# Loading and scaling of q, sums of tokens and scaling of v at the opening of a kernel's second level

## The chip, the core and the metric

The kernel runs on one core of a Trainium2 chip. The metric is the time of one execution on the device in microseconds (us), as the median of several runs. TensorE (PE; its weight loads PEld) multiplies and transposes, VectorE (DVE) and GpSimd (POOL) do arithmetic on tiles, ScalarE (ACT) copies and scales, SyncE (SP) issues DMAs. ScalarE and GpSimd also issue DMAs from their own queues. Each engine works through its own queue in order.

## The reference

Eight batches of eight heads, 576 tokens, 64 numbers a head; a retention block without softmax, and on its result a feed-forward block whose two branches are multiplied. All in float32.

```python
scores = scale * np.matmul(q, k.transpose(0, 1, 3, 2))
ret = scores * Dmat            # gamma_h ** (s - t) for t <= s, else 0
attn = np.matmul(ret, v)
x = attn.transpose(0, 2, 1, 3).reshape(B * S, H * D)   # 4608 x 512
a, b = x @ w1, x @ w2                                  # 512 x 1024 each
out = ((a * b) @ w3) @ w_out                           # 1024 x 1024, 1024 x 512
```

The decay is split: q is multiplied by gamma_h ** s / 8 and k's side (here v) by gamma_h ** -t before the products, so only a triangular mask is left for the scores.

## The kernel before

**Units of attention.** A unit `g` is a pair of batches (`i`) and a piece of the tokens (`c`): five pieces, the first of 64 tokens and four of 128, so 20 units; `NC` is 5. For each unit q and k are needed transposed (`qT`, `kT`), as 128 x (2 x 4 x 128) tiles; `score` (L233, L236) makes the masked scores, `state` (L255) adds k and v into a running state, `pv` (L274, L299) makes 128 columns of x, still transposed (`xT`).

There are two ways to `qT`. By **blocks**: `load_blocks` (L171) issues on SP up to 16 DMAs per unit, each of 32 KB, in runs of 32 numbers (128 bytes), so that every 32 x 32 block lies where a DVE block transpose finds it; `scale_blocks` (L181) multiplies by the decay on POOL in two instructions; `front_blocks` (L190) transposes on DVE. By **natural rows**: `load` (L93) issues one DMA in runs of 64 numbers (256 bytes); `scale` multiplies by the decay on POOL (L204) or head by head on ScalarE (L202, eight instructions); `front` transposes on TensorE (L218), eight instructions per tensor, into two PSUM tiles, which ScalarE copies out (L221).

**Feed-forward.** w3 @ w_out is multiplied out once (`w3o`). The products are Strassen-like (seven products for eight). Batches 0 to 3 use one level for the up products (`up`). From unit 10 on a second level is used: `up2(gr, n)`, 14 steps (`n` from 0 to 13) for each of four groups of two thirds-of-a-pair. I number the steps of a group from 1. A step is seven products of four matmul instructions each (L1035) on one weight form, which is fetched from HBM into a ring of three slots (`ra<-kept`, L939) by `next_forms`, mostly from POOL, two steps ahead. PSUM results go to the running sums `cc` by ScalarE copies (L1049, L1054, L1058, L1065), DVE sums (L1045, L1047) and POOL sums (`more`, L1040). Half-way through each step one entry of the list `beside` is run. `down` makes the output: seven products of eight matmul instructions (L637), with sums by DVE (`plus`, L641; S4 at L679; L681); P3, the last, needs S4 and the space of P5.

**Sums of tokens.** `token_forms(gr)` puts ten entries, each of one to three DVE instructions (L951), on a list. They make the second level's operands from `xT`. Step 1 needs the entries up to `outer`, step 3 the second-last, step 5 the last.

**The order of the work** is written out by hand: the program's text is the order on each engine, except that `work(n)` takes n pieces from the list `todo`, and small pieces wait in lists that other work empties: `spread` (one entry after each sum of `down` or `up`, all of them at `flush`), `aside` (after some sums), `beside` (in `up2`), `loads`. Before the second level, `open_second` and every `up2` call `flush`. Before the change, the ten entries for group 0 are on `spread`: four go out in `down` of tiles (2, 2) and (3, 2), and the other six at the `flush` in `open_second`, just ahead of `down` of (3, 0) and (3, 1), which is the last piece before step 1.

**Loops around the change.** After unit 9 there is a written-out passage for unit 10; then a loop over g from 10 to 19, in which `dealt[g - 10]` pieces of work (3, 4, 4, 3, 3, 7, 7, 3, 7, 7) are done, while unit g + 1 is prepared: v scaled by two entries of `beside` (four heads each), q scaled on POOL, q and k transposed after the second-last and last but one of the pieces, loads for g + 2 issued. At the end of the turn `pv(g)`, `state(g + 1)`, `score(g + 1)`. What is left in `beside` goes out before `pv`.

Of the kernel before, what the change touches and what calls it, by code (L numbers as in the profile page):

```python
# [13 lines left out]
ALU = mybir.AluOpType  # L14
# [5 lines left out]
def kernel(  # L20
# [16 lines left out]
    B, H, S, D = q.shape  # L37
# [10 lines left out]
    NC = (S + P - 1) // P  # L48
# [74 lines left out]
    for c in (0, slice(1, NC)):  # L123
        n = short if c == 0 else P
# [440 lines left out]
    aside, owed, spread, beside, loads = [], [], [], [], []  # L565
    g = 0
# [58 lines left out]
    def down(x, y, then=None, last=False):  # L625
        a, done, left = pair_of(x, y)
        second = "first" in live
        ahead(x, y)
        while len(done) < (1 if second else 3):
            aside.pop(0)()  # L630
        ps = {}
        ot = pools["ot"].tile([P, 2, 2, DM // 2], F32, tag="ot", name="ot")

        def product(nm, A, B, on=None):
            ps[nm] = ps[on] if on else acc.tile([P, DM // 2], F32, tag="acc", name="po")
            for f in range(NP):
                nc.tensor.matmul(ps[nm], a[A][:, f, :], live["W"][B][:, f, :], start=(f == 0 and not on),  # L637
                                 stop=(f == NP - 1), skip_group_check=True)

        def plus(nm, to, sb):  # L640
            nc.vector.tensor_add(ot[:, to[0], to[1]], ps[nm], ot[:, sb[0], sb[1]])  # L641
            if spread:
                spread.pop(0)()
            if second and aside and nm != 3:
                aside.pop(0)()

        def put(m, t, row, half=slice(0, 2)):

            i, n = every[m]
            r0 = t * P  # L650
            while r0 < (t + 1) * P:
                b = r0 // TB
                e = min((b + 1) * TB, (t + 1) * P)
                r = (2 * i + b) * S + n * TB + r0 - b * TB
                stores.append((out[r:r + e - r0, half.start * DM // 2:half.stop * DM // 2],
                               ot[r0 - t * P:e - t * P, row, half].rearrange("p h d -> p (h d)")))
                r0 = e
            if not keep_stores and not second:
                store()

        C11, C12, C21, C22 = (0, 0), (0, 1), (1, 0), (1, 1)
        product(1, "A11", "B11")
        first = ot[:, 0, 0]
        if second and steps[0]:
            first = live["first"].pop(0)
            live["first"].append(first)
        nc.scalar.copy(first, ps[1])
        if second:
            store()
            finish()  # L670
        product(7, "S3", "T3")
        if second:
            multiply()
        while len(done) < 3:
            aside.pop(0)()
        if then:
            ahead(*then)
        product(2, "A12", "B21", on=1)
        nc.vector.tensor_tensor(out=a["S4"], in0=a["A12"], in1=a["S2"], op=ALU.subtract)  # L679
        product(6, "S2", "T2")  # L680
        nc.vector.tensor_add(ot[:, 0, 1], ps[6], first)  # L681
        nc.scalar.copy(ot[:, 0, 0], ps[2])
        early = second or last or g >= 2 * NC - 1
        if early:
            put(*x, 0, slice(0, 1))
            store()
        plus(7, C21, C12)
        product(5, "S1", "T1")
        plus(5, C22, C21)
        product(4, "A22", "-T4")  # L690
        plus(4, C21, C21)
        put(*y, 1)
        if second:
            store()
        product(3, "S4", "B22", on=5)
        while aside and not early:
            aside.pop(0)()
        plus(3, C12, C12)
        put(*x, 0, slice(1 if early else 0, 2))
        if last:  # L700
            store()
        while aside:
            aside.pop(0)()

    stores, keep_stores = [], []

    def store():
        while stores:
# [102 lines left out]
    while multiplied[0] < KF:  # L811
# [3 lines left out]
        if todo:  # L815
            first = converted[0] < 4 * NQ
# [88 lines left out]
    def flush():  # L905
        while spread:
            spread.pop(0)()
# [34 lines left out]
    def token_forms(gr):  # L942


        x = [live["xT", m] for m in groups[gr]]
        T, E, U = live["T2"], live["E"], live["U"]
        forms = live["B2", gr] = {}
        names = ("B11", "B21", "B22", "T3", "T1", "T2", "-T4")

        def tt(out, in0, in1, op=ALU.subtract):  # L950
            nc.vector.tensor_tensor(out=out, in0=in0, in1=in1, op=op)  # L951

        b11, b21 = (x[0].rearrange("p (r c) b t -> p r c b t", c=2)[:, :, c] for c in range(2))
        b12, b22 = (x[1].rearrange("p (r c) b t -> p r c b t", c=2)[:, :, c] for c in range(2))

        def first():
            for s in range(2):
                tt(x[s][:, :2, 1], x[s][:, 2:, 1], x[s][:, :2, 1])


        def outer():
            if "E4" not in live:
                live["E4"] = pools["carry"].tile([P, KF, P], F32, tag="carry", name="e4").rearrange(
                    "p f n -> p (f n)")[:, :4 * TB].rearrange("p (r b t) -> p r b t", r=2, b=2)
            E4 = live["E4"]
            tt(E4, b21, E[:, 1])
            for nm, (r, b) in {"B11": (0, 0), "B21": (1, 0), "T3": (0, 1), "B22": (1, 1)}.items():
                parts = (b11, b21, b22, b12, E[:, 0], E[:, 1], E4)
                forms[nm] = dict(zip(names, (y[:, r, b] for y in parts)))

        def pair(k):
            for s in range(2):
                if k == 1:
                    tt(T[:, s, 1], x[s][:, :2, 1], x[s][:, :2, 0], ALU.add)
                else:
                    tt(T[:, s, k], x[s][:, 2:, 1 if k == 0 else 0], T[:, s, 1])

        def inner(k):
            u = [U[j] if k != 2 else (U[3][:, 0], U[3][:, 1], U[4][:, 0])[j] for j in range(3)]
            b11, b21, b12, b22 = (T[:, s, k, c] for s in range(2) for c in range(2))  # L980
            tt(u[1], b12, b11, ALU.add)
            tt(u[0], b22, u[1])
            tt(u[2], b21, u[1])
            for i, nm in enumerate(("T1", "T2") if k != 2 else ("-T4",)):
                part = [y[:, i] if k != 2 else y for y in (b11, b21, b22, b12, *u)]
                forms[nm] = dict(zip(names, part))

        spread.extend([first, lambda: tt(b12, b22, b12), lambda: tt(E[:, 1], b12, b11, ALU.add),
                       lambda: tt(E[:, 0], b22, E[:, 1])])
        spread.extend([lambda: pair(1), lambda: pair(0), lambda: pair(2), outer, lambda: inner(slice(0, 2)),  # L990
                       lambda: inner(2)] if gr else
                      [outer, lambda: pair(1), lambda: pair(0), lambda: pair(2), lambda: inner(slice(0, 2)),
                       lambda: inner(2)])
# [19 lines left out]

    def up2(gr, n):

        flush()
        h, key = n // 7, order[n % 7]
        slot = ring[steps[0] % 3]
        if not steps[0]:
# [108 lines left out]
    g = NC  # L1128
# [9 lines left out]
    for g in first_pair:  # L1138
        n = (1, 1, 2, 2)[g - NC]
# [37 lines left out]

    g = 2 * NC - 1
    work(1)
    load_blocks(g + 1, "q")  # L1180
    pv(g)()
    load(g + 2, "v", nc.scalar)
    load(g + 2, "k")
    scale_blocks(g + 1)
    scale(g + 1, "v")
    open_first()
    token_forms(0)

    g = 2 * NC
    work(1)  # L1190
    aside.append(lambda: front_blocks(g, "q"))
    work(1)
    while aside:
        aside.pop(0)()
    front(g, "k")
    next_forms(nc.scalar)
    ready = {2 * NC + 3: 1, 3 * NC + 1: 2, G - 1: 3}

    whole = range(2 * NC + 1, 2 * NC + 4)
    load_blocks(g + 1, "q")  # L1200
    state(g)
    score(g)
    add_group(0)
# [1 line left out]
    for g in range(2 * NC, G):  # L1205
        n = dealt[g - 2 * NC]
        if g + 1 < G:
            beside.extend(lambda j=j: scale(g + 1, "v", range(j, j + H // 2)) for j in (0, H // 2))
            tail = min(n, 4) - 3
            work(n - 2 - tail)  # L1210
            scale_blocks(g + 1)
            for nm in "qk":
                blocks_in = nm == "q" or g + 1 not in whole
                if blocks_in:
                    aside.append(lambda nm=nm: front_blocks(g + 1, nm))
                work(1)
                while aside:
                    aside.pop(0)()
                if not blocks_in:
                    while loads:  # L1220
                        loads.pop(0)()
                    front(g + 1, "k")
                if g + 2 < G and not (nm == "k" and g + 2 in whole):
                    load_blocks(g + 2, nm)
            work(tail)
            for left in (loads, beside):
                while left:
                    left.pop(0)()
        else:
            work(n)  # L1230
# [14 lines left out]
    g = G  # L1245
# [44 lines left out]
```

## Time and profile before

| | |
|---|---|
| median of 3 runs | 848.06 us (847.11 to 848.5) |
| the profiled execution | 856.03 us |
| its span, first to last instruction | 854.3 us |
| TensorE busy, of the span | 825.4 us (97%) |
| VectorE, ScalarE, GpSimd busy | 547.3, 282.8, 229.8 us |
| mean clock granted to TensorE | 0.988 |
| mean DMA rate | 149 GB/s |

The profile is that of one execution. A line of it names the engine, the line of the kernel, the operation, the tile written and those read (`out<-in`), the shape, the count. Matmuls are pipelined, and their ends are modelled. Times within the execution are counted from its first instruction.

### The profile page before, as it was taken

What the parts mean: (1) busy time and instruction counts of PE and PEld (TensorE: products, weight loads), DVE (VectorE), ACT (ScalarE), POOL (GpSimd) and SP (SyncE); (2) the same over time, 40 slices, a digit from 0 to 9 for tenths busy, and PEclk for the clock granted to TensorE, in tenths of its full rate; (3) what the DMA queues carried; (4) which work ended last, traced back from release to release, by engine and by line L of the source; (5) the groups of instructions that cost most, each with busy time, mean ns of one, the idle gap of its engine ahead of it and who ended that gap; (6) DMA issues with size and microseconds to landing.
All of it is one profiled execution on the core that took longest, in us unless ns stands there. A gap on an engine that the chain in (4) does not pass through costs nothing.

```text
span 854.3 us, 15755 instructions
## 1 busy us (share of the span) xinstructions
PE 825.4 (97%) x6085; PEld 743.0 (87%) x6085; DVE 547.3 (64%) x959; ACT 282.8 (33%) x581; POOL 229.8 (27%) x253
## 2 busy tenths in 40 slices
PE   9899999999999999986999999999999999999998
PEld 8899999644889898876999888999889998899987
DVE  4899999991654477943655862757654657645653
ACT  4787556670111011132453105342024231033300
POOL 1100010001103162203756103746005452035600
PEclk9999999999999999997999999999999999999999
DMA  9995464436046467987876427797446453145401
GB/s 190 217 218 132 76 149 124 126 96 111 1 95 124 74 179 265 262 257 153 236 198 186 100 65 176 229 228 209 77 90 201 158 193 132 49 138 188 167 26 50
DMA packets 201292, 126.96 MB, mean 149 GB/s; under 512 B 161272, under 2 KB 183032, under 8 KB 201216
## 3 DMA queue, kind: packets, MB, share of 16 engines
q1 hardware_dynamic: 170944, 50.14, 29.3%
q0 software_dynamic: 11632, 62.79, 22.7%
q10 hardware_dynamic: 18640, 13.02, 5.5%
q8 instruction: 48, 0.79, 0.4%
q14 instruction: 28, 0.23, 0.1%
HBM read 103.62 MB, written 22.28 MB: 147 GB/s over the span
## 4 chain that ended last, share of the span: by engine, by line
PE 81%; DMA 7%; DVE 6%; issue 3%; SPq 1%; ACT 1%; POOL 1%; ACTq 0%; DVEq 0%; POOLq 0%
PE po L637 23%; PE up L1035 15%; PE seed L1035 12%; PE up L524 12%; PE ps L477 6%; PE xps L299 4%; PE sc L233 3%; PE xps L274 2%; DMA ld_v<-in_v_dram 2%; DMA ra<-kept 2%; DMA raw<-in_moe_w_dram 2%; SPq L171 1%; PE tp L218 1%; DVE c L529 1%; PE st L255 1%
## 5 line engine op out<-in xcount | busy, mean ns | idle before, releaser
L637 PE MATMUL po<-w3o,ab 128*128 128x256 f32 x552 | 126.8, 385 | 5.4 <-DVE ot L641 4.4
L637 PEld LDWEIGHTS po<-w3o,ab 128*128 128x128 f32 x552 | 104.8, 192 | 22.7 <-DVE ot L641 6.7
L1040 POOL TENSOR_TENSOR cc<-cc 128x384 f32<-128x384 f32 x112 | 109.4, 1001 | 5.8 <-ACT cc L1058 4.1
L1047 DVE TENSOR_TENSOR cc<-seed,cc 128x384 f32<-128x384 f32 x88 | 48.7, 553 | 78.1 <-PE seed L1035 63.7
L1035 PE MATMUL up<-xT,ra 128*128 128x192 f32 x384 | 74.9, 332 | 0.5 <-DMA ra<-kept 0.5
L181 POOL TENSOR_TENSOR bl_q<-bl_q,gqs 128x512 f32<-128x512 f32 (+1 forms) x30 | 32.1, 1089 | 154.1 <-DMA bl_q<-in_q_dram 118.5
L1047 DVE TENSOR_TENSOR cc<-up,cc 128x384 f32<-128x384 f32 x88 | 48.5, 551 | 38.8 <-PE up L1035 30.7
L524 PE MATMUL up<-xT,wA 128*128 128x192 f32 x384 | 70.5, 327 | 0.0
L939 POOL DMA_DIRECT2D ra<-kept x53 | 30.0, 567 | 147.7 <-PE seed L1035 126.9
L529 DVE TENSOR_TENSOR c<-up,c 128x384 f32<-128x384 f32 x80 | 44.0, 549 | 39.7 <-PE up L524 39.1
L236 DVE TENSOR_TENSOR pm<-sc,mask 128x512 f32<-128x512 f32 (+1 forms) x80 | 45.4, 627 | 36.9 <-PE sc L233 36.8
L1035 PEld LDWEIGHTS up<-xT,ra 128*128 128x128 f32 x384 | 64.8, 193 | 1.8 <-DMA ra<-kept 0.8
L637 PE MATMUL po<-wB,forms 128*128 128x256 f32 x288 | 65.1, 379 | 0.0
L524 PEld LDWEIGHTS up<-xT,wA 128*128 128x128 f32 x384 | 63.3, 190 | 1.2 <-issue 0.5
L1035 PE MATMUL seed<-e,ra 128*128 128x192 f32 x256 | 52.5, 334 | 9.4 <-DVE cc L1047 6.9
L637 PEld LDWEIGHTS po<-wB,forms 128*128 128x128 f32 x288 | 54.7, 190 | 7.4
L1054 ACT COPY seed<-up 128x384 f32<-128x384 f32 x56 | 26.0, 463 | 96.1 <-PE up L1035 48.7
L1035 PE MATMUL up<-ra 128*128 128x192 f32 x288 | 56.1, 332 | 0.0
L477 PE MATMUL ps<-wo,w3T 128*128 128x512 f32 x128 | 55.1, 592 | 0.0
L1035 PEld LDWEIGHTS seed<-e,ra 128*128 128x128 f32 x256 | 43.0, 192 | 11.9 <-DVE cc L1047 7.2
L477 PEld LDWEIGHTS ps<-wo,w3T 128*128 128x128 f32 x128 | 24.3, 190 | 30.1 <-issue 29.7
L1035 PEld LDWEIGHTS up<-ra 128*128 128x128 f32 x288 | 49.3, 194 | 0.1
(126 smaller groups left out, 1477.5 us busy)
## 6 DMA issues: line engine op xcount, KB each, us to landing
ra<-kept POOLq DMA_DIRECT2D x53, 896.0 KB, 5.0
raw<-in_moe_w_dram SPq DMA_DIRECT2D x72, 128.0 KB, 3.0
bl_q<-in_q_dram SPq DMA_DIRECT2D x216, 32.0 KB, 2.8
out_dram<-ot ACTq DMA_DIRECT2D x54, 128.0 KB, 2.4
bl_k<-in_k_dram SPq DMA_DIRECT2D x136, 32.0 KB, 3.4
raw<-in_moe_w_dram SPq DMA_DIRECT2D x16, 256.0 KB, 6.7
ld_k<-in_k_dram SPq DMA_DIRECT2D x8, 512.0 KB, 5.6
raw<-in_moe_w_out_dram SPq DMA_DIRECT2D x32, 128.0 KB, 2.7
```

Source lines behind the costliest of these rows:

```text
L181: nc.gpsimd.tensor_tensor(out=part, in0=part, in1=gqs[:, :, n0:n0 + n].unsqueeze(3).to_broadcast([P, NP, n, BL]), op=ALU.mult)
L236: nc.vector.tensor_mul(pm[:sz, b, j, :, :sz], sc[j][:sz, :, :sz], mask[:sz, :sz].unsqueeze(1).to_broadcast([sz, NP, sz]))
L299: nc.tensor.matmul(banks[r][heads[half], b, n, :sz], vs[:sz, b * H + 2 * p + j, :], pm[:sz, b, j, p, :sz], start=(c == 0 and m == 0), stop ...
L477: nc.tensor.matmul(ps, live["w3T", ft][:, g, :], live["wo"][:, g, :], start=(g == 0), stop=(g == KF - 1))
L524: nc.tensor.matmul(ps[:, w, :], a[:, w, r, :], b[:, r, :], start=(new and w == r == 0), stop=(w == r == 1), skip_group_check=True)
L529: nc.vector.tensor_add(c[:, to], ps, c[:, sb])
L637: nc.tensor.matmul(ps[nm], a[A][:, f, :], live["W"][B][:, f, :], start=(f == 0 and not on), stop=(f == NP - 1), skip_group_check=True)
L939: engine.dma_start(ring[n % 3], kept[n % 14 // 7][nm])
L1035: nc.tensor.matmul(ps[:, w, :], weight_of(slot, a, w), B[b], start=(new and w == 0), stop=True, skip_group_check=True)
L1040: nc.gpsimd.tensor_tensor(out=o, in0=o, in1=i, op=ALU.add)
L1047: nc.vector.tensor_add(c[:, j], ps, with_add[:, j])
L1054: nc.scalar.copy(p6, p1)
```

## The change

Four edits, all in the order and the place of work; the values computed are the same.

- The ten entries of `token_forms` go on a list of their own, `pieces`. `down` takes one after each sum where `spread` is empty; `open_second` no longer empties them; `up2` leaves at most two before step 1, one before step 2, none before step 3.
- q of unit 10 is loaded by natural rows on SP, scaled on ScalarE (an entry of `aside`, taken in the last `down` before step 1), and transposed on TensorE together with k.
- q of unit 11 likewise; it is scaled by two entries of `beside` in steps 1 and 2, and transposed after step 3 with k.
- In every turn of the loop, the two entries that scale v go on `beside` after the first pieces of work of the turn, not before.

```diff
@@ down, plus @@
             if spread:
                 spread.pop(0)()
+            elif pieces:
+                pieces.pop(0)()
...
-    stores, keep_stores = [], []
+    stores, keep_stores, pieces = [], [], []
...
@@ token_forms @@
-        spread.extend([first, lambda: tt(b12, b22, b12), lambda: tt(E[:, 1], b12, b11, ALU.add),
+        pieces.extend([first, lambda: tt(b12, b22, b12), lambda: tt(E[:, 1], b12, b11, ALU.add),
                        lambda: tt(E[:, 0], b22, E[:, 1])])
-        spread.extend([lambda: pair(1), lambda: pair(0), lambda: pair(2), outer, lambda: inner(slice(0, 2)),
+        pieces.extend([lambda: pair(1), lambda: pair(0), lambda: pair(2), outer, lambda: inner(slice(0, 2)),
                        lambda: inner(2)] if gr else
...
     def up2(gr, n):
 
-        flush()
+
+        while len(pieces) > max(0, 2 - n):
+            pieces.pop(0)()
...
     g = 2 * NC - 1
     work(1)
-    load_blocks(g + 1, "q")
+    load(g + 1, "q")
     pv(g)()
     load(g + 2, "v", nc.scalar)
     load(g + 2, "k")
-    scale_blocks(g + 1)
     scale(g + 1, "v")
...
-    aside.append(lambda: front_blocks(g, "q"))
+    aside.append(lambda: scale(g, "q", True))
     work(1)
     while aside:
         aside.pop(0)()
-    front(g, "k")
+    front(g)
...
-    load_blocks(g + 1, "q")
+    load(g + 1, "q")
...
         if g + 1 < G:
-            beside.extend(lambda j=j: scale(g + 1, "v", range(j, j + H // 2)) for j in (0, H // 2))
+            q_blocks = g > 2 * NC
+            if not q_blocks:
+                beside.extend(lambda j=j: scale(g + 1, "q", range(j, j + H // 2)) for j in (0, H // 2))
             tail = min(n, 4) - 3
             work(n - 2 - tail)
-            scale_blocks(g + 1)
+            beside.extend(lambda j=j: scale(g + 1, "v", range(j, j + H // 2)) for j in (0, H // 2))
+            if q_blocks:
+                scale_blocks(g + 1)
             for nm in "qk":
-                blocks_in = nm == "q" or g + 1 not in whole
+                blocks_in = q_blocks if nm == "q" else g + 1 not in whole
                 if blocks_in:
                     aside.append(lambda nm=nm: front_blocks(g + 1, nm))
                 work(1)
                 while aside:
                     aside.pop(0)()
-                if not blocks_in:
+                if not blocks_in and nm == "k":
                     while loads:
                         loads.pop(0)()
-                    front(g + 1, "k")
+                    front(g + 1, "k" if q_blocks else "kq")
```

## The prediction

> **What bounds the kernel now.** I read the page first: TensorE's busy row, the clock row, the shares of the chain.
>
> ```profile
> PE 825.4 (97%) x6085; PEld 743.0 (87%) x6085; DVE 547.3 (64%) x959; ACT 282.8 (33%) x581; POOL 229.8 (27%) x253
> PEclk9999999999999999997999999999999999999999
> PE 81%; DMA 7%; DVE 6%; issue 3%; SPq 1%; ACT 1%; POOL 1%; ACTq 0%; DVEq 0%; POOLq 0%
> ```
>
> TensorE sets the end; only work taken from it, or a gap closed in it, counts. The one slice at a low clock is the 19th of 40, 384 to 406 us, where the second level opens. So next the busy time by stage (columns: stretch, its length, busy us and count of PE, PEld, DVE, ACT, POOL, clock, DMA share, GB/s): the last `down` before the second level, its first three steps, three later steps (from 404.9), and steps 1 and 2 of unit 15.
>
> ```profile
> 354.90:372.50 17.60, 14.27 (x57) 11.55 (x57) 14.15 (x23) 0.74 (x2) 4.42 (x3) 0.90 0.98 279
> 375.10:399.70 24.60, 17.71 (x87) 16.67 (x85) 5.91 (x12) 7.45 (x19) 7.15 (x8) 0.79 0.71 184
> 404.90:418.80 13.90, 13.90 (x88) 13.75 (x86) 8.71 (x15) 6.71 (x17) 10.34 (x12) 1.00 0.80 219
> 516.70:530.20 13.50, 11.38 (x60) 10.85 (x58) 3.03 (x8) 5.86 (x16) 3.83 (x5) 0.87 0.90 239
> ```
>
> Three steps take 13.90 us where nothing is late, 24.60 at the opening. The timeline of these stretches (start, length, engine, line, operation; in brackets the idle time before it and what ended it) tells why:
>
> ```profile
> 358.57 1.87 DVE L951 TENSOR_TENSOR ra<-xT 128x384 f32<-128x384 f32 x2
> 366.40 0.68 DVE L679 TENSOR_TENSOR ab<-ab,forms 128x512 f32<-128x512 f32 x1
> 368.86 3.68 PE L637 MATMUL po<-w3o,ab 128*128 128x256 f32 x8 [3.31 <-DVE ot L641]
> 372.66 27.75 SPq L171 DMA_DIRECT2D bl_q<-in_q_dram  x39
> 389.20 2.06 POOL L181 TENSOR_TENSOR bl_q<-bl_q,gqs 128x512 f32<-128x512 f32 x2 [26.99 <-DMA bl_q<-in_q_dram]
> 391.83 1.95 POOL L1040 TENSOR_TENSOR cc<-cc 128x384 f32<-128x384 f32 x2
> 392.87 0.56 DVE L1047 TENSOR_TENSOR cc<-seed,cc 128x384 f32<-128x384 f32 x1 [8.22 <-POOL cc L1040]
> 393.48 1.65 PE L1035 MATMUL seed<-e,ra 128*128 128x192 f32 x4 [6.89 <-DVE cc L1047]
> 396.20 2.76 PE L1035 MATMUL up<-ra 128*128 128x192 f32 x8
> ...
> 523.08 1.28 ACT L202 ACTIVATE ld_v<-ld_v,gk 128x128 f32<-128x128 f32 x4 [3.39 <-DMA ld_v<-in_v_dram]
> 525.15 0.95 PE L1035 MATMUL seed<-e,ra 128*128 128x192 f32 x4 [2.12 <-ACT seed L1054]
> 525.90 2.76 PE L1035 MATMUL up<-xT,ra 128*128 128x192 f32 x8
> ```
>
> Stall A (3.31 us): six sums of tokens, flushed together, hold DVE to 366.4; S4 and the sums of `down` queue behind them, and P3 waits for these. Stall B (6.89): POOL's head is the scaling of q of unit 11, whose sixteen block loads SP issues at 0.45 us each, after a stop:
>
> ```profile
> SPq L171 <- DMA ra<-kept: 5.5, 1, 5.5
> ```
>
> Behind it on POOL stand the form's DMA and the `more` sums of step 2; DVE and TensorE wait for those. Stall C (2.12): ScalarE waits for v of unit 16 in step 1, and the copy that seeds step 2 is behind it. After each, the same matmuls cost double for a while.
>
> **What the Trainium skill says.** "TensorE: Matmul & The Clock Gate", What's actually happening: an idle window of about 3.4 us halves the clock, and as much busy time restores it. The trace agrees: eight matmuls take 2.76 us after stalls B and C, 1.46 elsewhere. "SBUF — State Buffer", Who interferes with whom: a DVE instruction with two SBUF inputs is shut out while GpSimd reads SBUF. Here one DVE sum of 128x384 took 2.25 us at 360.4 while POOL scaled v of unit 10, its neighbours 0.55. "DMA: Bandwidth & Descriptors", Why small descriptors are slow: some 3 cycles per packet beside its 32-byte beats, so 256 B in two runs of 128 B cost 14, in one run 11. By that the new loads are about a fifth cheaper, an estimate; the trace has no such pair side by side.
>
> **The change, part by part,** in the profiled execution (856.03 us, span 854.3).
>
> Sums of tokens (A). The six leave 357.7 to 366.4. Four go one after each of the four L641 sums of that `down`, two to the starts of steps 2 and 3, where DVE was idle for 4.68 us before its first sum. POOL no longer scales q or (since its queue isn't blocked from 329 to 357.7) v there, so a dealt pair costs 2 x 0.55. Worked forward: P2 ends 360.4, S4 361.1, L681 at 362.2, sum 7 363.1, `outer` (0.95) 364.0, sum 5 364.4, a pair to 365.5, sum 4 366.0, a pair 367.1. P4 ends at 365.55, and P3 needs S4 and sum 5 only: no stall, and 1.99 instead of 3.68 us. That is 3.31 + 1.69 = 5.0 gained. If the dealt sums run as slowly as under POOL (0.97 each), sum 5 is at 365 and P3 still on time.
>
> q of unit 10. Off: 8 loads on SP (349.9 to 354.8), two scalings on POOL (2.25), one DVE transpose (0.70). On: one load; 8 multiplications by ScalarE after sum 7 (v of 64 rows: 8 in 2.45 us, 512.60 to 515.05), so 363.1 to 365.6, where ScalarE is idle; behind them stand only stores and the copies of `front`. 8 more transposes: the 8 of k took 0.63, so 0.6 on the path; two more copies (0.65), of which about 0.3 shows, since `state` (1.1) covers the rest and `score` wants the second. Cost 0.9. Four `front` tiles and four of `score` turn over five PSUM buffers; sum 3 (367.9) frees the fourth tile's in time. Net to here 4.1: step 1 begins at about 372.1, not 376.2.
>
> q of unit 11 (B). Off: 16 loads, POOL's 2.06, DVE's 1.23. On: one 512 KB load, 8 multiplications in fours (1.28 us) at the middle of steps 1 and 2, 8 transposes, 2 copies. SP's own order is kept, but the 24 loads are now 2; each load on SP or ScalarE waits for the landing of the one eight before it (the landings and issues pair off so in the trace), which was the 5.5 us stop. The load now follows the forms' load directly, at about 368 (the last send waits for the store behind L682, now about 367). k of unit 11, as large and natural, landed in 5.2 us at full DMA; with 1.8 MB of forms beside it I take 7: 375. ScalarE wants it at 372.1 + 3.1 = 375.2. So POOL has only forms and sums, and from the start of step 1 to `front` it takes 3 x 4.55 (a step's distance in the chain after 409.76) less the 0.65 of the product that comes later, 13.0, where it was 376.2 to 399.7, 23.5: 10.5 gained. Cost at the end of the stage: 8 transposes 0.87; ScalarE's four copies (2.3) and v's second half, which moving v one step leaves to after step 3 (1.28), end 4.0 us after `front` begins, when `state` wants v at 1.74 + 1.1 = 2.8: 1.0 more. Cost 1.9. SP then loads q of unit 12 some 12 us earlier; in 368 to 386 DMA has about 4.6 MB to move, 256 GB/s, under the 279 it moved in the first stretch.
>
> v by a step (C). Same eight multiplications, later: steps 2 and 3 of short units, 5 and 6 of those with seven, steps that already held POOL's scaling without loss in units of four. Unit 15: C and its slow clock are 2.12 + 1.95. But the forms of steps 3 and 4 land at 526.12 and 531.78, set by POOL and DMA, not by the wait; so step 4 begins at 531.8 instead of 534.1: 2.3 gained, not 4.1. Unit 18: the trace has step 2 at 5.18 instead of 4.55: 0.6. Unit 16: a form landing at 571.27 bounds it, 0.3.
>
> Sum: 4.1 + 10.5 - 1.9 + 2.3 + 0.6 + 0.3 = 15.9, so 840.1 for the profiled execution. The median of the runs is 848.06; the profiled one has 8 us more, and I can't see where. If a part of that is in these stalls, less is to be had; I take 14 off the median: 834.
>
> **Rivals.**
> R1, ScalarE takes over POOL's wait: q of unit 11 lands at 385, not 375, because two loads of forms share the DMA. For: those took 5.7 and 7.1 us there, and bl_q's first pieces up to 7.3. Against: SP reaches the load earlier, and half as many packets. TensorE then idles some 9.5 us; gain 15.9 - 9.5 = 6.4, so 841.7.
> R2, the runs without a profile hold most of their 8 us less in exactly these stalls: gain 8 to 9, 839.5. Nothing in the trace speaks for or against.
> R3, slower: the same wait on ScalarE, longer. It decides where q lands 15.9 us after ScalarE wants it, at 391 (388 if the slow clock's 3.3 us come on top). The last block of q landed at 389.2 before, so it takes a load as late as the blocks were. At 394 it is about 851. Against: the blocks' lateness was mostly issue and the stop of 5.5, both gone.
> R4, q wasn't the release: POOL is held by another load and B stays; A's gain is eaten by the 1.9 and 0.9. Within 0.2% of 848. Against: the bracket at 389.20 names the load.
>
> **How the numbers follow.** Forecast 834 (829 to 839): 0.62. R2: 0.11. R1: 0.16. R4: 0.03. R3: 0.08. The range to 843 takes in R1 and R2 and leaves out about 0.15. Faster by over 0.2% (what a measurement here can tell): 0.89; same 0.03; slower 0.08.
>
> **What would show it.** A: no gap over 1 us before the last product of the `down` ahead of step 1, its eight matmuls at about 2.0 us. B: POOL's first work after the opening is a form's DMA and `more`; steps 1 to 3 in 14 us; the clock row without its 7. A gap on ScalarE before L202 on ld_q would be R1 or R3. C: no wait for ld_v at L202 in unit 15, but one for ra of about 1 us in TensorE at its steps 3 and 4. I am wrong if step 3 still ends 20 us or more after the seeds, or if a new gap over 2 us stands before `state` of unit 11.

## The result and the profile after

The changed kernel takes 839.28 us (median of four runs) where the kernel before takes 847.72 on the same chip. The gain is 8.4 us; 14 were forecast. One of the four runs, the profiled one, was disturbed (a span of 942.5 us at a clock of 0.846) and is left out of the ratio, which is 0.9891 with a 95% interval of 0.9868 to 0.9914; the median of the other three is 838.87 us.

All that is shown of "after" therefore comes from a second profile of the same kernel, `all_again`: its span is 837.3 us, its own run 838.99 us.

The page of that profile: busy time by engine, the clock row in 40 slices, the shares of the chain.

```profile
PE 819.1 (98%) x6101; PEld 736.9 (88%) x6101; DVE 544.1 (65%) x957; ACT 289.8 (35%) x601; POOL 225.4 (27%) x249
PEclk8999999999999999999999999999999999999999
PE 76%; DMA 10%; DVE 4%; SPq 4%; issue 3%; ACT 2%; POOL 1%; ACTq 0%; DVEq 0%; POOLq 0%
```

The 7 in the clock row is gone, and TensorE has the 16 transposes more that q of two units needs (6101 for 6085). The busy time by stage, with the columns as in the prediction: the last `down`, steps 1 to 3, and the stretch from the transposes of unit 11 to step 4.

```profile
350.90:368.90 18.00, 16.28 (x137) 13.88 (x137) 9.97 (x19) 4.88 (x15) 0.00 (x0) 0.98 0.98 291
371.50:385.40 13.90, 13.54 (x82) 12.98 (x81) 6.01 (x13) 8.47 (x23) 4.77 (x6) 1.00 0.85 198
385.40:392.00 6.60, 6.60 (x114) 5.98 (x112) 2.79 (x6) 4.34 (x11) 1.59 (x2) 1.00 0.61 167
```

Steps 1 to 3 take 13.9 us instead of 24.6, at full clock. POOL does nothing in the `down` (0.00): it has no q to scale there, and v of unit 10, which stood behind q on POOL, is scaled at 328.47 us instead of 359.99. Lines of the timeline of the same kernel (line numbers are two to four higher than before):

```profile
354.98 0.37 ACT L669 COPY ot<-po 128x256 f32<-128x256 f32 x1 [7.93 <-DMA out_dram<-ot]
355.40 1.99 PE L637 MATMUL po<-w3o,ab 128*128 128x256 f32 x8 [0.74 <-ACT ot L669]
...
362.42 1.89 PE L637 MATMUL po<-w3o,ab 128*128 128x256 f32 x8
364.68 1.02 DVE L953 TENSOR_TENSOR ra<-xT,ra 128x384 f32<-128x384 f32 x2
365.32 1.12 ACTq L712 DMA_DIRECT2D out_dram<-ot  x2
366.48 0.65 ACT L221 COPY kT<-tp 128x256 f32<-128x256 f32 x2 [3.49 <-DVE ra L953]
367.46 1.46 PE L233 MATMUL sc<-qT,kT 64*64 64x64 f32 x32 [0.93 <-ACT qT L221]
368.85 2.87 PE L1027 MATMUL seed<-w3o,ident 128*128 128x384 f32 x4
376.02 1.28 ACT L202 ACTIVATE ld_q<-ld_q,gq 128x128 f32<-128x128 f32 x4 [1.62 <-DMA ld_q<-in_q_dram]
378.04 0.62 POOL L941 DMA_DIRECT2D ra<-kept  x1 [47.63 <-DVE u L953]
378.10 0.92 PE L1039 MATMUL seed<-e,ra 128*128 128x192 f32 x4 [0.36 <-ACT seed L1058]
378.67 1.99 POOL L1044 TENSOR_TENSOR cc<-cc 128x384 f32<-128x384 f32 x2
388.27 1.78 PE L255 MATMUL st<-ld_v,ld_k 128*64 128x64 f32 x32
513.15 0.89 PE L1039 MATMUL up<-ra 128*128 128x192 f32 x4 [0.49 <-DMA ra<-kept]
```

Stall A is gone: the last product (362.42) has no bracket, and its eight matmuls take 1.89 us where they took 3.68. Stall B is gone from POOL, whose first work after 47.63 idle us is a form's DMA, then `more`. In its place ScalarE waits 1.62 us for q of unit 11, and 0.36 of them reach TensorE. Stall C has become waits of half a microsecond for a weight form. New are the 0.74 at 355.40, behind a ScalarE copy that waits for the landing of a store of `ot` (none in the first profile of before, 0.32 in the second), and the 0.93 before the scores: these wait for ScalarE's copies of `front`, which stand on ScalarE behind two stores issued at 365.32.

Where the time went is read best between fixed points: from the start of the scores of one unit (first L233 matmul) to the next. Before unit 9 the executions differ by several microseconds whatever the kernel; the table leaves that out.

| stage, us | before | before, second profile | after |
|---|---|---|---|
| scores of unit 9 to those of 10 | 49.5 | 47.8 | 47.0 |
| unit 10 to 11 | 29.0 | 29.4 | 22.5 |
| these two: the opening | 78.5 | 77.2 | 69.5 |
| unit 15 to 16 | 39.1 | 39.1 | 35.8 |
| unit 16 to 17 | 40.0 | 41.1 | 40.1 |
| unit 18 to 19 | 37.4 | 36.8 | 36.7 |

The gain lies in the opening (7.7 to 9.0 us) and in unit 15 (3.3). Single executions differ in the opening too: a kernel below whose opening is that of before (`v_only`) has 75.6 us there, 6.1 more than after. So stages of two profiles add up to more than the medians' 8.4, and I use them to say where, not how much.

### The profile page after: what moved, and what is told of

It reads as the page before. It is cut to its first block, busy times and chain, and to the rows that moved or that the text cites. A ratio compares the mean times of both kernels' runs of the same rounds, so it can differ in the third digit from the quotient of the medians.

```text
span 942.5 us, 15780 instructions
## 1 busy us (share of the span) xinstructions
PE 931.7 (99%) x6101; PEld 818.4 (87%) x6101; DVE 545.4 (58%) x957; ACT 289.7 (31%) x601; POOL 224.4 (24%) x249
## 4 chain that ended last, share of the span: by engine, by line
PE 95%; DMA 3%; SPq 1%; ACT 0%; POOL 0%; issue 0%; DVE 0%; ACTq 0%
PE po L637 26%; PE up L524 18%; PE up L1039 18%; PE seed L1039 13%; PE ps L477 7%; PE xps L299 4%; PE sc L233 4%; PE xps L274 2%; PE st L255 2%; PE tp L218 1%; DMA ld_v<-in_v_dram 1%; DMA kept<-wA 1%; DMA ld_q<-in_q_dram 1%; DMA out_dram<-ot 1%; SPq L93 0%; SPq L342 0%
## 5 line engine op out<-in xcount | busy, mean ns | idle before, releaser
L637 PE MATMUL po<-w3o,ab 128*128 128x256 f32 x552 | 145.0, 426 | 2.8 <-ACT ot L669 2.2
L1039 PE MATMUL up<-xT,ra 128*128 128x192 f32 x384 | 83.7, 360 | 0.0
L524 PE MATMUL up<-xT,wA 128*128 128x192 f32 x384 | 80.5, 360 | 0.0
L637 PE MATMUL po<-wB,forms 128*128 128x256 f32 x288 | 75.8, 425 | 0.0
L524 PEld LDWEIGHTS up<-xT,wA 128*128 128x128 f32 x384 | 72.0, 197 | 1.4 <-issue 0.6
L1039 PEld LDWEIGHTS up<-xT,ra 128*128 128x128 f32 x384 | 72.0, 198 | 1.3 <-issue 0.4
L236 DVE TENSOR_TENSOR pm<-sc,mask 128x512 f32<-128x512 f32 (+1 forms) x80 | 45.4, 627 | 41.2 <-PE sc L233 41.1
L477 PE MATMUL ps<-wo,w3T 128*128 128x512 f32 x128 | 64.4, 673 | 0.0
L1039 PE MATMUL up<-ra 128*128 128x192 f32 x288 | 62.5, 359 | 0.0
L1039 PEld LDWEIGHTS up<-ra 128*128 128x128 f32 x288 | 54.6, 198 | 0.2
L524 PE MATMUL up<-T,wS 128*128 128x192 f32 x256 | 53.5, 359 | 0.0
```

Source lines behind the costliest of these rows:

```text
L236: nc.vector.tensor_mul(pm[:sz, b, j, :, :sz], sc[j][:sz, :, :sz], mask[:sz, :sz].unsqueeze(1).to_broadcast([sz, NP, sz]))
L477: nc.tensor.matmul(ps, live["w3T", ft][:, g, :], live["wo"][:, g, :], start=(g == 0), stop=(g == KF - 1))
L524: nc.tensor.matmul(ps[:, w, :], a[:, w, r, :], b[:, r, :], start=(new and w == r == 0), stop=(w == r == 1), skip_group_check=True)
L1039: nc.tensor.matmul(ps[:, w, :], weight_of(slot, a, w), B[b], start=(new and w == 0), stop=True, skip_group_check=True)
```

## The experiments

**The change and its three parts.** My theory: A (sums dealt), B (q by rows) and C (v moved) each remove a stall of their own. The rivals: one part does it all, or the parts stand in for each other. `all_again` and `before_again` are the two kernels unchanged.

> The changed kernel once more, for a profile at full clock and more runs. Theory (three stalls closed one by one): 838 to 839 us as measured; in the profile no gap over 1 us before the last product of the down ahead of step 1, 13 to 15 us from step 1 to the transposes of unit 11, no wait for ld_v in unit 15. Rival (ScalarE has taken over the wait for q): the same time, with a gap on ScalarE before the multiplication of ld_q in step 1.

Measured: 839.09 us (837.56 to 844.97), ratio 0.9902 [0.9876, 0.9929].

> The kernel before once more, for a second profile: the first was of an execution 8 us over the median. Theory (that execution was slow at the opening by chance, since its DMAs are saturated there): 846 to 850 us, from the scores of unit 9 to those of unit 11 some 75 us (78.5 in the first profile, 69.5 in the changed kernel), unit 15 as in the first profile within 1 us. Rival (a profile costs 8 us): 855 us or more again.

Measured: one run at 852.11, span 850.4, between the two guesses; the kernel before in the same session had a median of 848.57. Its gaps are those of the first profile: 2.72 us before the last product, 6.71 in step 2, 2.10 in unit 15. One thing differs. In `before_again` the last product runs at full speed behind its gap (clock 1.00), in 1.99 us and not in 3.68:

```profile
365.75 1.99 PE L637 MATMUL po<-w3o,ab 128*128 128x256 f32 x8 [2.72 <-DVE ot L641]
```

`sums_only`, the sums alone:

```diff
@@ plus; token_forms (both lists); up2 @@
+            elif pieces:
+                pieces.pop(0)()
-        spread.extend([...
+        pieces.extend([...
-        flush()
+        while len(pieces) > max(0, 2 - n):
+            pieces.pop(0)()
```

> Only the sums of tokens dealt one by one, the rest as before. Theory: the stall of 3.3 us and its slow clock go, 4 to 5 us less, 843 to 844 us, the stall on q of unit 11 stays at 6 to 7 us. Rival (the forms' and the stores' DMAs set the opening, not VectorE): the end of that down comes earlier, and the stall on q of unit 11 grows by as much, no change, 847 to 848 us.

Measured: 847.74, ratio 0.9999 [0.9986, 1.0013]. No gain at all, as the rival had it. The timeline of `sums_only` in the opening:

```profile
370.38 0.92 PE L1038 MATMUL seed<-e,ra 128*128 128x192 f32 x4 [1.11 <-ACT seed L1057]
375.84 0.89 PE L1038 MATMUL up<-xT,ra 128*128 128x192 f32 x4 [2.59 <-DMA ra<-kept]
383.85 2.06 POOL L181 TENSOR_TENSOR bl_q<-bl_q,gqs 128x512 f32<-128x512 f32 x2 [27.81 <-DMA bl_q<-in_q_dram]
388.14 1.65 PE L1038 MATMUL seed<-e,ra 128*128 128x192 f32 x4 [4.53 <-DVE cc L1050]
```

Stall A is gone there too, and the steps begin earlier; but then they wait for a copy (1.11), a weight form (2.59), and POOL with its blocks of q (4.53). The opening takes 77.8 us, as before. What did not move forward is SP's queue. On it stand the sends, the DMAs that take the weight forms of the second level's second half to HBM, then the load of a weight form into the space that the sends read, then the blocks of q. That load leaves SP at 368.93, just after the last send from this space has landed (368.73), and the first block behind it at 369.37. ScalarE issues a form's load at 368.98 that waits for the same landings; the late copy (1.11) is behind it.

`q_only`, q of both units by rows:

```diff
@@ unit 9's turn, unit 10's turn, the loop @@
-    load_blocks(g + 1, "q")
+    load(g + 1, "q")
-    scale_blocks(g + 1)
-    aside.append(lambda: front_blocks(g, "q"))
+    aside.append(lambda: scale(g, "q", True))
-    front(g, "k")
+    front(g)
-    load_blocks(g + 1, "q")
+    load(g + 1, "q")
+            q_blocks = g > 2 * NC
+            if not q_blocks:
+                beside.extend(lambda j=j: scale(g + 1, "q", range(j, j + H // 2)) for j in (0, H // 2))
...
```

> Only q of units 10 and 11 by natural rows, ScalarE and TensorE; sums as before, v scaled in the steps as before (q ahead of it in unit 10's turn). Theory: the stall of 6.9 us and its slow clock go, less the cost of transposes and copies, 7 to 8 us less, 840 to 841 us; the stall of 3.3 us before the last product of the down stays. Rival (ScalarE waits for q in POOL's place): 844 us or more, with a wait of 5 us or more before the multiplication of ld_q.

Measured: 842.21, ratio 0.9926 [0.9902, 0.995], a little short of the 840 to 841 expected; the opening takes 69.8 us. Of the timeline of `q_only`, the wait in the last `down`:

```profile
360.79 0.37 ACT L667 COPY ot<-po 128x256 f32<-128x256 f32 x1 [10.01 <-DMA out_dram<-ot]
361.22 2.62 PE L637 MATMUL po<-w3o,ab 128*128 128x256 f32 x8 [2.83 <-ACT ot L667]
```

The last product (369.92) shows no gap although the sums are flushed as before: TensorE had already waited 2.83 us for space held by a store, and DVE did the flush in that time. Two late things overlapped.

`v_only`, the scaling of v alone:

```diff
-            beside.extend(... "v" ...)
             tail = min(n, 4) - 3
             work(n - 2 - tail)
+            beside.extend(... "v" ...)
```

> Only the scaling of v moved behind the first pieces of each turn, the rest as before. Theory: unit 15's 2.1 us gap goes, but the landing of the forms bounds steps 3 and 4, and unit 18 gains 0.6: 2 to 3 us less, 845 to 846 us. Rival (the forms' landing takes all of it, or in runs without a profile v has landed in time): 847.5 to 848 us.

Measured: 847.23, ratio 0.9994 [0.998, 1.0007]. In the timeline of `v_only` the wait for v in unit 15 is gone, and the forms' landings have taken its place:

```profile
518.05 0.89 PE L1035 MATMUL up<-ra 128*128 128x192 f32 x4 [0.55 <-DMA ra<-kept]
523.53 0.76 PE L1035 MATMUL up<-xT,ra 128*128 128x192 f32 x3 [0.69 <-DMA ra<-kept]
```

Unit 15 takes 36.8 us there for 39.1, the predicted 2.3; the median allows at most 1.7.

**Combinations.** `sums_q` has the edits of `sums_only` and `q_only` together, so it is the change without C.

> Sums dealt one by one and q by natural rows; v scaled in the steps as before. Theory (sums gain nothing alone, since the block loads of q end the stall behind them at the same time, but gain with q by rows): 839 to 840 us, that is 2 to 3 us under q alone, and no more than 1 us over the whole change. Rival (sums gain nothing at all, v does it): 842 us as q alone.

Measured: 839.08, ratio 0.989 [0.9871, 0.9909]: the time of the whole change. Against `q_only` that is 3.1 us less, but the intervals of the two overlap, and their profiles differ by only 0.6 us in the opening (69.8 and 69.2). So that the sums add something to q is likely, and not shown.

Unit 15 of `sums_q` takes 36.4 us with v where it was. In `q_only`, `sums_q` and `q11_only` v lands 6.4 to 6.5 us after the scores of unit 15, against 7.4 to 7.6 in both profiles of before and in `sums_only`. Why is not settled: in the changed kernel itself it lands at 7.8, and in `light_before` below, with q in blocks, at 6.7.

`q11_only` leaves q of unit 10 in blocks and takes only unit 11 by rows:

```diff
@@ unit 10's turn; the loop as in q_only @@
-    load_blocks(g + 1, "q")
+    load(g + 1, "q")
+            q_blocks = g > 2 * NC
...
```

> Only q of unit 11 by natural rows; q of unit 10 by blocks, sums and v as before. Theory (POOL's wait for the blocks of unit 11 is the whole of what q gains, and unit 10 by rows only costs transposes): 841 to 842 us, as q of both. Rival (the eight loads of unit 10 hold SP up and so the landing of q of unit 11): 844 to 845 us, with a wait on ScalarE for ld_q in step 1 of over 2 us.

Measured: 845.41, ratio 0.9965 [0.9954, 0.9976]. Half of what `q_only` gains. The timeline of `q11_only`:

```profile
369.47 0.43 SPq L93 DMA_DIRECT2D ld_q<-in_q_dram  x1
379.24 1.28 ACT L202 ACTIVATE ld_q<-ld_q,gq 128x128 f32<-128x128 f32 x4 [5.97 <-DMA ld_q<-in_q_dram]
381.31 1.65 PE L1035 MATMUL seed<-e,ra 128*128 128x192 f32 x4 [3.70 <-ACT seed L1054]
```

This is rival R1 as the prediction wrote it: ScalarE waits for q (5.97 us), its seeding copy stands behind, TensorE idles 3.70. The load leaves SP at 369.47, which is 49.5 us after the scores of unit 9. In `q_only`, which differs from this kernel in unit 10 alone, it leaves 44.7 us after them, and ScalarE does not wait. So whether unit 10 is loaded in blocks, eight small loads ahead on SP, decides whether R1 comes about.

**Is it the number of loads, or the sends?** The stretch of the last `down` is also when the sends (6.4 MB) go out, and DMA is busy all through. The `light` kernels leave these sends out and read the first half's forms in their place; part of the computation is thus missing, and their times serve this comparison alone. Leaving them out frees two things at once, DMA and SP's queue.

```diff
@@ weight_forms, send @@
+            if h == 1:
+                return
@@ next_forms @@
-            engine.dma_start(ring[n % 3], kept[n % 14 // 7][nm])
+            engine.dma_start(ring[n % 3], kept[0][nm])
```

`light_before` is the kernel before with this, `light_sums` and `light_q` add one part, `light_all` the whole change.

> The kernel before without the 6.4 MB of sends of the second half's weight forms (its forms are read from the first half's place, so the result is not the reference's): DMA is freed just ahead of and in the opening. Theory (saturated DMA sets the opening): the scores of unit 9 to those of unit 11 fall from 77 to about 72 us and the time to 842 to 844 us, since loads and stores land sooner; the wait for the sums before the last product of the down stays at about 3 us. Rival (SP's rate of issue and VectorE's sums set it): 846 us or more.

> The same without those sends (result not the reference's), with the sums dealt one by one. Theory (with DMA free, the 4 to 5 us that the sums were to gain are to be had): 4 to 5 us under the same kernel without it. Rival (the blocks of q of unit 11, issued by SP one by one, still end the next wait at the same time): no change against it.

> The same without those sends (result not the reference's), with q of both units by natural rows and sums and v as before. Theory: 6 to 8 us under the kernel before without the sends; the stall before the last product of the down, 2 to 3 us, is there again. Rival (with DMA free the blocks are as good): under 3 us.

> The same without those sends (result not the reference's), with the whole change. Theory (the change lost its gain on the sums to late landings): 12 to 15 us under the kernel before without the sends, the opening at 66 us or less and no gap over 0.5 us in it. Rival (what was lost isn't lost to DMA): 8 to 9 us under it, as with the sends.

| | median, us | ratio to before [95%] | opening, us | the same with the sends |
|---|---|---|---|---|
| `light_before` | 841.81 | 0.9912 [0.9882, 0.9942] | 69.7 | 849.72; 77.2 |
| `light_sums` | 838.89 | 0.988 [0.9851, 0.9909] | 66.6 | 847.74; 77.8 |
| `light_q` | 844.41 | 0.9926 [0.9903, 0.9949] | 72.9 | 842.21; 69.8 |
| `light_all` | 839.58 | 0.9877 [0.9843, 0.9911] | 66.6 | 839.09; 69.5 |

Without the sends the old loads are in time, and the kernel before gains nearly as much as the change brings (849.72 to 841.81). Busy time in the stretch 360 to 370 us (last two columns: DMA share, GB/s), first `before_again`:

```profile
360.00:370.00 10.00, 7.28 (x90) 6.02 (x90) 6.48 (x16) 1.02 (x3) 0.00 (x0) 1.00 0.95 304
```

then `light_before`:

```profile
360.00:370.00 10.00, 7.52 (x46) 5.82 (x46) 6.11 (x15) 1.12 (x3) 0.00 (x0) 0.83 0.48 105
```

and from the timeline of `light_before`, the last product and POOL's scaling of q of unit 11:

```profile
365.42 2.70 PE L637 MATMUL po<-w3o,ab 128*128 128x256 f32 x8 [2.48 <-DVE ot L641]
376.48 2.06 POOL L181 TENSOR_TENSOR bl_q<-bl_q,gqs 128x512 f32<-128x512 f32 x2 [17.71 <-DMA bl_q<-in_q_dram]
```

The same sixteen block loads are complete at 376.48, not at 385.16 as in `before_again`, and stall B does not occur; stall A (2.48) stays. It is not that the loads meet less traffic and run faster: from the first of them to POOL's scaling it takes 22.0 us here and 14.8 in `before_again`. They are in time because SP comes to them 16 us earlier. SP's issues in `before`, ahead of the blocks of unit 11 (372.66):

```profile
355.63 1.92 SPq L939 DMA_DIRECT2D ra<-kept  x1
357.66 3.15 SPq L882 DMA_DIRECT2D kept<-wA  x4
360.91 3.67 SPq L885 DMA_DIRECT2D kept<-wS  x1
364.62 3.08 SPq L882 DMA_DIRECT2D kept<-wA  x4
367.75 4.08 SPq L888 DMA_DIRECT2D kept<-wS  x2
372.27 0.34 SPq L939 DMA_DIRECT2D ra<-kept  x1
```

and the blocks in `light_before`:

```profile
354.49 38.31 SPq L171 DMA_DIRECT2D bl_q<-in_q_dram  x43
```

So the blocks were late because eleven sends, and a form's load that waits for them to land, stand ahead of them on SP. That their pace is DMA's is likely (a share of 0.95 from 360 to 370 us), but not shown apart.

q by rows then brings nothing: `light_q` is 2.6 us above `light_before`, with overlapping intervals. It was expected 6 to 8 us under it, and `light_all` 12 to 15, which is only 2.2 under it: `light_before` has no stall B left to remove. The profile of `light_q` shows what is late instead:

```profile
358.35 3.78 PE L637 MATMUL po<-w3o,ab 128*128 128x256 f32 x8 [3.44 <-ACT ot L667]
```

Again a copy of the last `down` waits for a store's landing; q and two forms go out early here, and DMA is full from 350 to 360 us without the sends too (a share of 1.15). And dealing out the sums is worth 2.9 us here (841.81 to 838.89), or 4.8 on top of q (844.41 to 839.58), close to the 5.0 predicted. The intervals of these pairs overlap; the profiles (opening 69.7 to 66.6, 72.9 to 66.6) point the same way.

**A version that goes on from there.** `better` keeps the change and holds the two stores of the last `down` back to step 1, so that ScalarE's copies for `front` are not behind them; it scales the second half of v in step 3.

```diff
@@ down @@
-        if second:
+        if second and steps[0]:
             store()
@@ up2 @@
+        if steps[0] == 3 and beside:
+            beside.pop(0)()
```

> The whole change, and the stores behind the second-last sum of the last down before step 1 left to step 1, so that they don't hold ScalarE's copies of the transposes; the second half of v of unit 11 scaled in step 3, not after it. Theory (the gap of 0.93 us before the scores of unit 10 comes from those stores' wait): that gap and up to 1.3 us of slow clock behind it go, and 0.6 us before the state of unit 11: 836.5 to 838 us. Rival (the copies then wait for something else, or the stores end later and hold SP's load of forms): 839 us or more.

Measured: 838.3 (836.2 to 841.58), ratio 0.9877 [0.9854, 0.9899]: not to be told from the change. The timeline of `better`:

```profile
366.98 1.56 PE L1027 MATMUL seed<-w3o,ident 128*128 128x384 f32 x4
369.28 5.27 ACTq L712 DMA_DIRECT2D out_dram<-ot  x3
374.59 0.48 ACT L1062 COPY cc<-up 128x384 f32<-128x384 f32 x1 [4.91 <-DMA out_dram<-ot]
375.12 1.27 PE L1039 MATMUL up<-xT,ra 128*128 128x192 f32 x3 [3.82 <-ACT cc L1062]
```

The gap before the scores is gone, and the seeding products take 1.56 us again, as was to be expected if the stores cause both. But the stores now occupy ScalarE in step 1 (4.91 us without a copy), and TensorE waits 3.82 us there. The gap has moved, and the opening is no shorter (71.8 us).

## Why the prediction was right, and where not

**The direction and the range held**, in part by luck. The forecast itself, 834 with 829 to 839, was missed by a little (839.3); the time lies in the part of the range, up to 843, that was left for R1 and R2. It is the one that R2 gave (839.5), but R2's reason explains only a part of it: the sum was too high in A, and too low in unit 15 (3.3 us gained for 2.3).

**The extra 8 us of the profiled execution** were mostly elsewhere. In `before_again` and `v_only`, which have the same opening, it takes 77.2 and 75.6 us, not 78.5, while the time ahead of unit 9 is 321.4 and 319.2 us for 324.5. So 1 to 3 of the 8 us were in the stalls: R2's point in small.

**A, "3.31 + 1.69 = 5.0 gained".** The working of the `down` was right to a few tenths: no stall, 1.89 us for the product, and a dealt pair of sums in 1.02 us for the 1.1 assumed. Two things failed. The 1.69 for the slow clock were of one execution: in `before_again` the product behind the stall takes 1.99 us, so there are 2.8 us to close there and not 5.0. And the step from there to the end fails. Alone the part measures 0 (0.9999), on top of q some 3 (842.21 to 839.08, with overlapping intervals), and with the sends gone 2.9 and 4.8. I had let everything after the `down` move forward with it; the forms and the blocks of q did not, because they stand on SP behind the sends and wait until these have landed. The prediction's check that 256 GB/s is less than 279 was a mean over 18 us, and the waits are at single landings.

**q of unit 10, "cost 0.9".** The first step begins 20.6 us after the first product of the last `down`, not 17.2. The 3.4 us are 0.74 for P2 (a copy that waits for a store), 0.93 before the scores, 0.36 as these run 1.46 us instead of 1.10, and 1.31 as the seeding products run at half clock (2.87 us for 1.56). "Behind them stand only stores" was true, and the stores were what mattered: a store that waits for the landing of another DMA holds the copies behind it on ScalarE. This gap is not in every execution: in `sums_q` and `q_only` the same copies are in time, and the seeding products take 1.56 us.

**B, "10.5 - 1.9".** Right in size: steps 1 to 3 take 13.8 us for 13.0, and the stretch from the transposes to step 4 takes 6.6 for 5.1, so 1.5 against the 1.9 charged, of which `state` makes 0.63 (1.78 for 1.15). The landing at 375.9, from an issue at 367.05, meets the forecast of 368 to 375. R1 came in small, 1.62 us on ScalarE of which 0.36 reach TensorE. But two things were not seen. The gain needs both units: with unit 10 in blocks it halves, by R1's mechanism. And "the blocks' lateness was mostly issue and the stop of 5.5" is only a part of the cause. It fits what follows the first of the loads, 14.8 us in `before_again` where the one load by rows lands 8.9 us after its issue. The other part is when SP comes to the first of them, after the sends: without these, the same number of issues is complete at 376.48.

**The sum of the opening**: 4.1 + 8.6 = 12.7 predicted, 6.1 to 9.0 between the profiles. Only `light_sums` and `light_all`, with the sends gone, come near the 65.8 us that the prediction implies (66.6 in both).

**C, "2.3 + 0.6 + 0.3".** The new waits for forms were as forecast in place, and half as long (0.49 to 0.69 for about 1). In unit 15 the profile shows the 2.3. But in `q_only`, with v where it was, unit 15 takes 36.4 us too, so on top of it C is worth 0.6 in the profile and nothing in the median (839.08 and 839.09). The 0.6 of unit 18 is not C's, since `before_again` has it too (36.8 us), and of the 0.3 in unit 16 nothing shows. That `v_only`'s median shows less than its profile's 2.3 is left open.

**R3 and R4.** No run came near R3's 851: q landed 1.6 us after ScalarE wanted it, not 15.9. R4 is excluded by `q_only`.

## What to carry to other kernels

When several stalls follow one another and each has its own engine at the bracket, ask for each what it would wait for next, before adding up the gains. Here stall A stood at VectorE and stall B at POOL. Removing A alone gained nothing, because what comes next hangs on SP's queue, where 6.4 MB of sends stand ahead; without the sends it gained 2.9 us by the medians. So parts of a change are judged together and apart. Ask too how much of a stall is in every execution: of the 5.0 us of A, 1.69 were a slow clock that a second profile did not have. And a mean DMA rate with room in it does not say that the next load is in time; look at issue and landing of the one that the path needs, and at what stands before it on the queue that issues it.

## What the hardware did unexpectedly

- A DMA on ScalarE's queue that has to wait holds the arithmetic behind it. In `better`, ScalarE had no copy for 4.91 us behind three stores; the last of them went out at 374.18 us, when q of unit 11 had landed (374.10). In `all_again` the first of the two stores ahead of `front`'s copies went out at 365.32, when a send had landed (365.24). The trace tells why: all DMAs of SP and ScalarE signal one of eight semaphores, and each waits until the DMA that used its semaphore before has landed. So it is a wait that the program contains, and not a full queue. The prediction had seen it in SP's issues, and not asked what it does on an engine that also computes. "DMA: Bandwidth & Descriptors", Issuing engines are not separate DMA queues, in the Trainium skill, says that DMAs of all issuing engines end in the same 16 DMA engines; what ties a store of ScalarE to a load of SP in these two cases is the shared semaphore.
- The clock fell to half after a gap of only 0.93 us. In `all_again` the four seeding products took 2.87 us (granted clock 0.50), in `q_only` after the same 16 transposes but without a gap 1.56. The length of a gap does not decide by itself: after 2.72 us in `before_again` the product ran at clock 1.00 (1.99 us), after 2.20 us in `sums_q` at 0.52 (3.68 us). "TensorE: Matmul & The Clock Gate", What's actually happening, in the Trainium skill, gives an idle window of about 3.4 us; these gaps are shorter, and so was stall C (2.12), which the prediction took for agreement. Part 4 of the same page says that transposes do not count as busy in the same way, which would fit the first case, but no run here separates the two.
- With POOL idle in the `down`, a DVE sum of 128x384 took 0.51 us (two in 1.02), where one beside POOL's scaling had taken 2.25.
